# Routing attention and a squared-ReLU MLP on one core: the nine score tiles of a head pair in one run, its nine v products in another, and small transposes moved from TensorE to VectorE

## The chip, the cores and the metric

The kernel runs on one core of a Trainium2 chip. The time is device microseconds (us) of one launch, the median of several runs. Engines are named as the profile names them: PE (TensorE matmul) and PEld (its weight loads), DVE (VectorE), ACT (ScalarE), POOL (GpSimd) and SP (SyncE), whose queue issues nearly all DMAs in program order.

## The reference

Attention over 4 batches, 8 heads, 768 positions of 64 values; keys and queries see each other only if they fall to the same one of 16 clusters. An MLP follows.

```python
q_assign = argmax(einsum(q_n, c_n)); k_assign = argmax(einsum(k_n, c_n))
mask = q_assign[:, :, :, None] == k_assign[:, :, None, :]
scores = where(mask, scale * q @ k.T, -1e9)
attn = exp(scores - max); attn = attn / (sum(attn) + 1e-09)
x = (attn @ v) as (3072, 512)
out = square(maximum(x @ w_in, 0)) @ w_out        # 512 -> 2048 -> 512
```

## The kernel before, in words

**Attention** goes by pairs: two heads of a batch share the 128 partitions (64 values each), so there are NG = 16 pairs, p = 0 to 15. A pair's work on PE is: `logits` (L314; products with the centroids), `turn_logits` (L327; three 128x128 transposes), nine score tiles `sc` of 128 x 2 x 512, each made of products q.k (L435, f32) and of a mask product with one-hot cluster numbers `ohT` (L446, bf16), then 18 products with v (L521, into the bank `av`), and `add_up` (L533; sums of the exponentials over the keys, into `sm`). ACT makes each tile's exponential `ex` (L453, straight from PSUM) and evicts `av` into `xT` (L527). DVE and POOL add the exponentials of a pair into `total` (all under L456); DVE finds the cluster numbers from the logits (`number`, L347 to L360), inverts the sums (L543), multiplies x by them (`finish`, L556), and makes `ohT` (`one_hot`, L404 and L407).

A loop over t = 0 to 48 steps through thirds of pairs (p, ph = divmod(t, 3)): each step makes three score tiles, and then the v products of the step *before* it. Every engine runs in the order of the program text in this part (`manual_schedule`, closed at L688), so the text sets what is queued behind what.

Three things go through DRAM, all by SP. The raw q and k of pair p+3 are split into 16-bit halves by ACT (`flat`, L295), written (`words`, L296) and read back transposed (`qkT`, L307). The cluster numbers of a pair are written (`far`, L393) and read back spread over 2 x 64 partitions (`wide`, L396). The inverse sums are written (`far_r`, L546) and read back spread (`rb`, L549). Pairs 0 to 2 take their one-hots and pairs 0 and 1 their q, k by PE transposes instead.

PSUM: three score tiles of two banks each (`ps_sc`), one bank `av` (`ps_av`) and one bank for everything small (`ps_m`, "m").

**Weights** come in 32 blocks of 512 KB (16 of w_in, 16 of w_out), loaded into three buffers (L135) and rounded: `round_1` on ACT (L143, L144), `round_2` on DVE (L150, L153, L157), `round_3` on POOL (L165). Sixteen are rounded during attention, sixteen during the first `up`.

**The MLP** works by batches in the order 1, 2, 3, 0, each as `up` (L737: 8 groups of 7 products of 4 matmul rows, L748) and `down` (L766: 3 blocks of 7 products, L781), Strassen-like: sums of operands are made beforehand on POOL (`w_sums`, L586 and L566) and DVE (`x_sums`), and each product's bank is added into its results by DVE (`combine`, L723). Eight banks are in use here. In the first `up`, the hook `behind_group` adds up, inverts and finishes pair 15 and rounds two weight blocks in each group; before the first `down` the four sums `w_t` of w_out are made on DVE. From L688 on a scheduler orders the instructions.

Of the kernel before, what the change touches and what calls it, by code (L numbers as in the profile page):

```python
# [25 lines left out]
def kernel(  # L26
# [23 lines left out]
    NT = 3 * NG  # L50
# [13 lines left out]
    endp = ending.enter_context(tc.tile_pool(name="endp", bufs=2, side="right"))  # L64

    loads = att.enter_context(tc.tile_pool(name="loads", bufs=6))
# [5 lines left out]
    expp = att.enter_context(tc.tile_pool(name="expp", bufs=6))  # L72
# [11 lines left out]
    BY_PE, ONE_HOT = 2, 3  # L84
# [128 lines left out]
    seen = const.tile([4 * NG, TB], F32, name="seen")  # L213

    oh = once.tile([P, NB, 4, 2, D], BF16, name="oh")
    nc.gpsimd.memset(oh, 0.0)

# [96 lines left out]
    def logits(pair):  # L314
        hp = pair % HP
        lg = misc("lg", [P, TB], spare=pair == 0)
        for g in range(4):
            nc.tensor.matmul(  # L318
                lg[32 * g : 32 * g + 32], lhsT=cnT[:, 2 * C * hp : 2 * C * (hp + 1)],
                rhs=qkT[pair][:, NB * g : NB * (g + 1)], start=True, stop=True,  # L320
            )
        lgs[pair] = once.tile([P, TB], F32, name="lgs")
        nc.scalar.copy(out=lgs[pair], in_=lg)

    lts = {}

    def turn_logits(pair):  # L327
        lts[pair] = misc("lt", [P, NB, P])
        src = lgs.pop(pair)
        for i in range(NB):  # L330
            nc.tensor.transpose(  # L331
                out=lts[pair][:, i], in_=src[:, i * P : (i + 1) * P], identity=ident
            )

    numbers = {}

    def number(pair):
        n = NB * P // C
        mx = small.tile([P, n], F32, name="mx")
        best = once.tile([P, n, C], BF16, name="best")  # L340
        first = small.tile([P, n], F32, name="first")
        lt = lts.pop(pair).rearrange("p i (g c) -> p (i g) c", c=C)

        def over_c(t):
            return t.unsqueeze(2).to_broadcast([P, n, C])

        nc.vector.reduce_max(out=mx, in_=lt, axis=AX.X)  # L347
        nc.vector.tensor_tensor(out=best, in0=lt, in1=over_c(mx), op=ALU.is_ge)
        nc.vector.tensor_tensor(
            out=best, in0=best, in1=order.unsqueeze(1).to_broadcast([P, n, C]), op=ALU.mult  # L350
        )
        nc.vector.reduce_max(out=first, in_=best, axis=AX.X)
        if pair < ONE_HOT:
            nc.vector.tensor_tensor(
                out=oh.rearrange("p i g e c -> p (i g e) c")[:, :, 0:C], in0=best,
                in1=over_c(first), op=ALU.is_equal,
            )
        else:
            numbers[pair] = small.tile([P, 2, 4, NB], BF16, name="ids_b")
            nc.vector.tensor_copy(  # L360
                out=numbers[pair].rearrange("p e g i -> p i g e"),
                in_=first.rearrange("p (i g e) -> p i g e", i=NB, g=4),
            )

    def turn_onehot(pair):
        ohT[pair] = ohtp.tile([P, 2, S], BF16, name="ohT")
        for which in range(2):
            pt = misc("po", [P, NCH, P], BF16, spare=which == 0)
            for c in range(NCH):
                nc.tensor.transpose(  # L370
                    out=pt[:, c],
                    in_=oh[:, c % NB, 2 * which + c // NB].rearrange("p e c -> p (e c)"),
                    identity=ident_b,
                )
            dst = ohT[pair][:, which]
            src = pt.rearrange("p c n -> p (c n)")
            if which == 0:
                nc.vector.tensor_copy(out=dst, in_=src)
            else:
                nc.scalar.activation(out=dst, in_=src, func=ACT.Copy, bias=-BIG, scale=BIG)  # L380

    wide = {}

    def spread(pair):
        n = 8 * NB
        pb = misc("pb", [n, P], BF16)
        nc.tensor.transpose(
            out=pb, in_=numbers.pop(pair).rearrange("p e g i -> p (e g i)"), identity=ident_b
        )
        row = small.tile([n, P], BF16, name="row")  # L390
        far = dram.tile([2, n // 2, P], BF16, name="far")
        nc.scalar.copy(out=row, in_=pb)
        nc.sync.dma_start(far.rearrange("e r n -> (e r) n"), row)  # L393
        wide[pair] = once.tile([P, 2, S], BF16, name="wide")
        for e in range(2):
            nc.sync.dma_start(  # L396
                wide[pair][D * e : D * (e + 1)].rearrange("p g n -> p (g n)"),
                far[e].rearrange("r n -> (r n)").partition_broadcast(D),
            )

    def one_hot(pair):
        ohT[pair] = ohtp.tile([P, 2, S], BF16, name="ohT")
        src = wide.pop(pair)
        nc.vector.tensor_scalar(  # L404
            out=ohT[pair][:, 0], in0=src[:, 0], scalar1=cl, scalar2=None, op0=ALU.is_equal
        )
        nc.vector.tensor_scalar(  # L407
            out=ohT[pair][:, 1], in0=src[:, 1], scalar1=cl, scalar2=-BIG,
            op0=ALU.not_equal, op1=ALU.mult,
        )  # L410
# [6 lines left out]
    total = {}  # L417

    def pieces(t):
        pair, ph = divmod(t, 3)  # L420
        if ph < 2:
            rounds = [[(i, 3 * ph + i, slice(0, QA)) for i in range(3)]]
            queries = slice(0, QA)
        else:
            rounds = [[(i, 2 * i + j, slice(QB * j, QB * (j + 1))) for i in range(3)]
                      for j in range(2)]
            queries = slice(QA, S)
        return pair, rounds, queries

    def score_products(t, todo):  # L430
        pair, _, queries = pieces(t)
        for i, c, cols in todo:
            for e in range(2):
                rows = slice(D * e, D * (e + 1))
                nc.tensor.matmul(  # L435
                    sc[t][i][:, e, cols], lhsT=qkT[pair][rows, NCH + c],
                    rhs=qkT[pair][rows, queries.start // P : queries.stop // P],
                    start=True, stop=False,
                )

    def mask_products(t, todo):
        pair, _, queries = pieces(t)
        for i, c, cols in todo:
            for e in range(2):
                rows = slice(D * e, D * (e + 1))
                nc.tensor.matmul(  # L446
                    sc[t][i][:, e, cols], lhsT=ohT[pair][rows, 1, c * P : (c + 1) * P],
                    rhs=ohT[pair][rows, 0, queries], start=False, stop=True,
                )

    def exponential(t, i):
        ex.setdefault(t, []).append(expp.tile([P, 2, 512], F32, name="ex"))
        nc.scalar.activation(out=ex[t][i], in_=sc[t][i], func=ACT.Exp, scale=SCALE)  # L453
# [3 lines left out]

    part = {}

    def add_first(pair):  # L460
        e0, e1, e2 = ex[3 * pair]
        total[pair] = endp.tile([P, 2, S], F32, name="total")
        dst = total[pair][:, :, 0:QA]
        add(nc.vector, dst, e0, e1)
        add(nc.vector, dst, dst, e2)

    def add_second(pair):
        e0, e1, e2 = ex[3 * pair + 1]
        part[pair] = accp.tile([P, 2, 512], F32, name="part")
        add(nc.gpsimd, part[pair], e0, e1)  # L470
        add(nc.gpsimd, part[pair], part[pair], e2)

    def merge_second(pair):
        dst = total[pair][:, :, 0:QA]
        add(nc.vector, dst, dst, part.pop(pair))

    third = {}

    def add_third(pair):
        e0, e1, e2 = ex[3 * pair + 2]  # L480
        part[pair] = accp.tile([P, 2, 512], F32, name="part")
        add(nc.gpsimd, part[pair], e0, e1)
        third[pair] = e2

    def merge_third(pair):
        p = part.pop(pair)
        add(nc.vector, p, p, third.pop(pair))
        add(nc.vector, total[pair][:, :, QA:S], p[:, :, 0:QB], p[:, :, QB : 2 * QB])

    def begin(t):  # L490
        sc[t] = [ps_sc.tile([P, 2, 512], F32, name="sc") for _ in range(3)]

    def scores(t):
        begin(t)
        pair, rounds, _ = pieces(t)
        for todo in rounds:
            score_products(t, todo)
            if t % 3 == 0 and pair < ONE_HOT:
                turn_onehot(pair)
            mask_products(t, todo)  # L500
# [9 lines left out]
    def times_v(t):  # L510
        pair, rounds, queries = pieces(t)
        ph = t % 3
        if ph != 1:
# [522 lines left out]
```

## Time and profile before

| | us |
|---|---|
| median of 3 runs | 968.41 (966.81 to 968.68) |
| the profiled execution, own time | 964.27 |
| its span, first to last instruction | 962.4 |
| PE busy | 928.6 (96%) |
| DVE, ACT, POOL busy | 564.5, 319.9, 269.9 |
| granted TensorE clock, mean | 0.990 |
| attention, pair 0 to the first product of `up` | about 12 to 365.5 |
| first `up`, then first `down` | 365.5 to 447.4, to 522.4 |
| each later `up` and `down` | 72.24 and 72.52 |

In a timeline of the profile, a row has the start in us from the span's start, the duration in us, engine, line, operation, the tiles out<-in, the shape and how many instructions were merged; in brackets stands the idle time of the engine before it and what ended that. A PE row "64*128 64x512" is one pass of a matmul with 64 rows and 128 columns; an f32 matmul is two passes.

### The profile page before, as it was taken

The numbers are of one execution on the slowest core, as the hardware profiler recorded it, in microseconds if no ns is written. First come the engines' busy times: TensorE is split into PE (matmuls) and PEld (weight loads), VectorE is DVE, ScalarE is ACT, GpSimd is POOL, SyncE is SP. The second block draws the span as 40 slices with busy tenths as digits, with TensorE's granted clock in tenths as the row PEclk, the third lists the DMA queues.
The fourth block names the chain that finished last, engine by engine and source line by source line (L and its number), as shares of the span: only waits on it lengthen the run. The fifth ranks groups of instructions, "written<-read, shape, count | busy, mean of one in ns | idle before, by whom it ended". The sixth has DMA issues, their size and how long they took to land.

```text
span 962.4 us, 11697 instructions
## 1 busy us (share of the span) xinstructions
PE 928.6 (96%) x4556; PEld 585.8 (61%) x4556; DVE 564.5 (59%) x794; ACT 319.9 (33%) x491; POOL 269.9 (28%) x217
## 2 busy tenths in 40 slices
PE   8989999999999959988999999999999999999997
PEld 4444444444444425545887556887556888556886
DVE  5577886676668976988232666332666332666331
ACT  4757676666666534654000111000111000111000
POOL 0233444333444564671002320002321002321000
PEclk9999999999999988999999999999999999999999
DMA  6867787897775212421000000000000000000000
GB/s 199 229 136 183 193 237 191 211 209 191 197 194 160 94 40 73 146 84 65 22 22 23 0 1 1 23 22 22 1 0 1 22 22 22 0 1 1 22 23 26
DMA packets 97715, 79.66 MB, mean 83 GB/s; under 512 B 53493, under 2 KB 86645, under 8 KB 97397
## 3 DMA queue, kind: packets, MB, share of 16 engines
q1 hardware_dynamic: 95940, 78.41, 29.8%
q8 instruction: 38, 0.62, 0.3%
q10 hardware_dynamic: 1712, 0.43, 0.2%
q14 instruction: 25, 0.20, 0.1%
HBM read 48.66 MB, written 19.05 MB: 70 GB/s over the span
## 4 chain that ended last, share of the span: by engine, by line
PE 81%; DVE 8%; issue 4%; ACT 2%; DMA 2%; POOL 2%; ACTq 0%; SPq 0%; DVEq 0%; POOLq 0%
PE bank L781 29%; PE bank L748 23%; PE sc L435 11%; PE av L521 11%; PE sc L446 3%; DVE g L723 1%; PE lg L318 1%; PE sm L537 1%; DMA w_raw<-in_moe_w_out_dram 1%; DVE total L456 1%; DVE w_raw L150 1%; POOL w_out L165 1%; PE lt L331 1%; DVE w_raw L153 1%; DVE w_t L566 1%
## 5 line engine op out<-in xcount | busy, mean ns | idle before, releaser
L453 ACT ACTIVATE ex<-sc 128x1024 f32<-128x1024 f32 x144 | 140.2, 1025 | 87.6 <-PE sc L446 87.6
L723 DVE TENSOR_TENSOR g<-bank,g 128x384 f32<-128x384 f32 x192 | 103.5, 554 | 92.6 <-PE bank L748 89.1
L521 PE MATMUL av<-ex,v_raw 128*64 128x512 f32 (+1 forms) x768 | 137.0, 500 | 10.1 <-ACT xT L527 10.0
L435 PE MATMUL sc<-qkT 64*128 64x512 f32 (+1 forms) x768 | 140.9, 499 | 0.0
L456 POOL TENSOR_TENSOR part<-ex 128x1024 f32<-128x1024 f32 x32 | 77.2, 2412 | 206.5 <-ACT ex L453 180.9
L781 PE MATMUL bank<-w_out,g 128*128 128x256 f32 x576 | 127.2, 379 | 2.0 <-DVE g L566 2.0
L586 POOL TENSOR_TENSOR w_s<-w_in 128x256 f32<-128x256 f32 x32 | 26.3, 821 | 360.6 <-PE bank L781 242.0
L781 PEld LDWEIGHTS bank<-w_out,g 128*128 128x128 f32 x576 | 109.4, 190 | 18.1 <-DVE g L566 2.4
L723 DVE TENSOR_TENSOR osb<-bank,osb 128x256 f32<-128x256 f32 x72 | 29.5, 423 | 145.5 <-PE bank L781 134.9
L435 PEld LDWEIGHTS sc<-qkT 64*128 64x128 f32 x768 | 69.4, 188 | 56.4 <-issue 39.9
L521 PEld LDWEIGHTS av<-ex,v_raw 128*64 128x64 f32 x768 | 51.9, 139 | 80.4 <-issue 48.0
L748 PE MATMUL bank<-x_t,w_s 128*128 128x384 f32 x256 | 93.3, 487 | 1.8 <-POOL w_s L566 1.0
L748 PE MATMUL bank<-xT,w_in 128*128 128x384 f32 x256 | 93.8, 489 | 0.7 <-DVE g L723 0.7
L748 PE MATMUL bank<-xT,w_s 128*128 128x384 f32 x256 | 93.1, 486 | 1.2 <-DVE g L723 1.2
L781 PE MATMUL bank<-w_t,g_s 128*128 128x256 f32 x384 | 86.8, 379 | 0.0
L781 PE MATMUL bank<-w_t,g 128*128 128x256 f32 x384 | 86.8, 379 | 0.0
L781 PEld LDWEIGHTS bank<-w_t,g_s 128*128 128x128 f32 x384 | 73.0, 190 | 9.9
L781 PEld LDWEIGHTS bank<-w_t,g 128*128 128x128 f32 x384 | 73.0, 190 | 9.9
L727 ACT COPY osb<-bank 128x256 f32<-128x256 f32 x12 | 4.5, 372 | 213.5 <-PE bank L781 213.5
L748 PEld LDWEIGHTS bank<-x_t,w_s 128*128 128x128 f32 x256 | 48.4, 190 | 36.7 <-POOL w_s L566 1.6
L727 ACT COPY g<-bank 128x384 f32<-128x384 f32 x32 | 15.2, 475 | 165.4 <-PE bank L748 165.4
L748 PEld LDWEIGHTS bank<-xT,w_s 128*128 128x128 f32 x256 | 48.5, 190 | 35.5 <-DVE g L723 2.3
(122 smaller groups left out, 1057.6 us busy)
## 6 DMA issues: line engine op xcount, KB each, us to landing
words<-flat SPq DMA_DIRECT2D x28, 384.0 KB
w_raw<-in_moe_w_in_dram SPq DMA_DIRECT2D x16, 512.0 KB
w_raw<-in_moe_w_out_dram SPq DMA_DIRECT2D x16, 512.0 KB
v_raw<-in_v_dram SPq DMA_DIRECT2D x16, 384.0 KB
rb<-far_r SPq DMA_DIRECT2D x32, 192.0 KB
out_dram<-osb SPq DMA_DIRECT2D x23, 256.0 KB
q_raw<-in_q_dram SPq DMA_DIRECT2D x14, 384.0 KB
k_raw<-in_k_dram SPq DMA_DIRECT2D x14, 384.0 KB
```

Source lines behind the costliest of these rows:

```text
L150: nc.vector.scalar_tensor_tensor(out=lo, in0=hi, scalar=0x80000000, in1=lo, op0=ALU.bitwise_and, op1=ALU.bitwise_or)
L153: nc.vector.tensor_scalar(out=hi.bitcast(F32), in0=dst.bitcast(F32), scalar1=2.0 ** -15, scalar2=HIGHEST, op0=ALU.max, op1=ALU.min,)
L435: nc.tensor.matmul(sc[t][i][:, e, cols], lhsT=qkT[pair][rows, NCH + c], rhs=qkT[pair][rows, queries.start // P : queries.stop // P], start ...
L446: nc.tensor.matmul(sc[t][i][:, e, cols], lhsT=ohT[pair][rows, 1, c * P : (c + 1) * P], rhs=ohT[pair][rows, 0, queries], start=False, stop= ...
L453: nc.scalar.activation(out=ex[t][i], in_=sc[t][i], func=ACT.Exp, scale=SCALE)
L456: eng.tensor_tensor(out=out, in0=a, in1=b, op=ALU.add)
L521: nc.tensor.matmul(av[pair][D * e : D * (e + 1), 0:n], lhsT=raw_v[pair][:, e, c], rhs=e_t[i][:, e, cols], start=c == 0, stop=c == NCH - 1,)
L586: nc.gpsimd.tensor_tensor(out=s1, in0=a[1][0], in1=a[1][1], op=ALU.add)
L723: nc.vector.tensor_tensor(out=out, in0=bank, in1=to, op=ALU.add)
L727: nc.scalar.copy(out=c11, in_=bank)
L748: nc.tensor.matmul(bank, lhsT=operands[j][0][:, kk], rhs=operands[j][1][:, kk], start=(kk == 0), stop=(kk == H2 - 1),)
L781: nc.tensor.matmul(bank, lhsT=operands[j][0][:, f], rhs=operands[j][1][:, f], start=(f == 0), stop=(f == F2 - 1),)
```

## The change

1. **Order of a pair.** The loop goes by pairs. Tiles 0 to 5 (`tile_of`) are made one after another, each q.k product followed by its mask product; tiles 6 to 8 as before in two halves; then the v products of all nine. `expp` has 9 buffers instead of 6 (`loads` 5 instead of 6, `endp` 1 instead of 2). The second `av` bank is the small bank "m". Then come `logits` of pair p+2 and `add_up` of p itself.
2. **Transposes by DVE.** The logits are turned by DVE from PSUM in blocks of 32 x 32 (L335 of the changed kernel), without ACT's copy `lgs` and PE's `lt`. The cluster numbers are turned by DVE (L355), without PE's `pb` and ACT's `row`. The sums are turned by DVE and only one column in 32 is inverted (128x12 in place of 128x384). `wide` is filled for 16 of each 64 partitions; its buffer, and the inverses `seen`, are written in place, so that the copy `seen<-r` falls away. `far` and `far_r` become 128 rows of 64 and 48 bytes. Only pair 0 takes its one-hots by PE.
3. **Adds.** POOL adds tiles 0+1 and 3+4+5, DVE the rest; `finish` of pair p-1 stands in pair p between two adds of DVE, as two instructions, one for each half of the columns.
4. **Weights.** `round_1` of block p in pair p, `round_2` and `round_3` in pair p+1: one block in each pair, loaded two pairs ahead. 17 blocks are left for the first `up` (3, 3, 2, 2, 2, 2, 2, 1 by group).
5. **First `up` and first `down`** stay in the order of the text, until the first block of `down` is done. `round_1` stands behind the eviction of a group's first product, the squares of a group (all by ACT) in the next group, `w_sums` two groups ahead; the four sums `w_t` stand between the products of `down`.

The core of the loop after (the adds, weight rounds and the branches for p = 0 are cut):

```diff
+    for p in range(NG):
+        load_qk(p + 3)
+        load_ahead(0)
+        if p:
+            turn_words(p + 2)
+        load_v(p + 1)
...
+        if 2 < p + 1 < NG:
+            number(p + 1)
+        if p:
+            invert(p - 1)
...
+            for i in range(NB):
+                tile_of(p, i)
...
+        for i in range(NB, NCH):
+            tile_of(p, i)
...
+        split_words(p + 3, 0)
...
+        for i in range(NCH, NCH + NB):
+            exponential(i)
+        add(nc.vector, first, first, part)
+        if p:
+            finish(p - 1)
+            round_3(p - 1)
...
+        add(nc.vector, part, ex[NCH], ex[NCH + 1])
+        add(nc.vector, part, part, ex[NCH + 2])
+        add(nc.vector, last, part[:, :, 0:QB], part[:, :, QB : 2 * QB])
+        round_1(p)
...
+        bank = av_bank("av")
+        for i in range(NCH):
+            times_v(p, i, bank)
+        evict(p, 0, bank)
+        split_words(p + 3, 1)
+        bank = misc("av", [P, 512])
+        for i in range(NCH, NCH + NB):
+            times_v(p, i, bank)
+        raw_v.pop(p)
+        if 2 < p + 2 < NG:
+            logits(p + 2, misc("lg", [P, TB], spare=True))
+        evict(p, NCH, bank)
+        if p + 1 < NG:
+            add_up(p, misc("sm", [P, TB]))
+            one_hot(p + 1)
```

and what `add_up` left in PSUM is inverted one pair later:

```diff
+    def invert(pair):
+        turned = endp.tile([P, NBL, 32], F32, name="sums_t")
+        nc.vector.transpose(out=turned.rearrange("p b i -> p (b i)"), in_=sums.pop(pair))
+        r = seen[:, NBL * pair : NBL * (pair + 1)]
+        nc.vector.reciprocal(out=r, in_=turned[:, :, 0])
+        far = dram.tile([2, P // 2, NBL], F32, name="far_r")
+        nc.sync.dma_start(far.rearrange("e i b -> (e i) b"), r)
+        rb = endp.tile([P, 2, 32, NBL], F32, name="rb")
```

In the first `up`:

```diff
+            def behind_copy():
+                if waiting:
+                    squares(waiting.pop(), True)
+                rounding(i, 1)
...
+        if stage == 2 and i == 0:
             add_up(NG - 1, bank_tile(TB))
+            invert(NG - 1)
             finish(NG - 1)
```

## The prediction, made before the result was known

> **What bounds it now.** The page first: PE is busy 96% of the span and holds 81% of the chain that ended last, so I look for PE time saved and for the places where PE stood still.
>
> ```profile
> PE 928.6 (96%) x4556; PEld 585.8 (61%) x4556; DVE 564.5 (59%) x794; ACT 319.9 (33%) x491; POOL 269.9 (28%) x217
> PE 81%; DVE 8%; issue 4%; ACT 2%; DMA 2%; POOL 2%; ACTq 0%; SPq 0%; DVEq 0%; POOLq 0%
> ```
>
> Then PE's timeline. In mid attention it has no idle time; the pattern of 207.32 returns at 228.01, so a pair costs 20.69 us.
>
> ```profile
> 207.32 0.55 PE L331 MATMUL lt<-ident,lgs 128*128 128x128 f32 x3
> 207.80 2.85 PE L435 MATMUL sc<-qkT 64*128 64x512 f32 x12
> 210.48 0.81 PE L446 MATMUL sc<-ohT 64*128 64x512 bf16 x6
> 211.22 0.23 PE L387 MATMUL pb<-ident_b,ids_b 128*24 128x128 bf16 x1
> 211.38 2.81 PE L521 MATMUL av<-ex,v_raw 128*64 128x256 f32 x24
> ...
> 217.54 0.85 PE L537 MATMUL sm<-total,ups 128*32 128x384 f32 x8
> ```
>
> At the end of attention it stands still, in the same view, and ACT's timeline says why: an eviction is queued behind `round_1`, which waits for a weight block.
>
> ```profile
> 347.41 2.79 PE L521 MATMUL av<-ex,v_raw 128*64 128x512 f32 x12
> 360.21 5.39 PE L521 MATMUL av<-ex,v_raw 128*64 128x256 f32 x24 [10.01 <-ACT xT L527]
> 365.53 1.76 PE L748 MATMUL bank<-xT,w_in 128*128 128x384 f32 x4
> ```
>
> ```profile
> 359.04 0.65 ACT L144 ACTIVATE w_raw<-w_raw 128x512 f32<-128x512 uint32 x1 [8.88 <-DMA w_raw<-in_moe_w_out_dram]
> ```
>
> The 24 passes at 360.21 take 5.39 where 2.81 is usual: the granted clock of 340 to 380 is 0.83. The first `up` takes 365.53 to 447.40 = 81.87 against 72.24 later; the first `down` 74.95 against 72.52.
>
> Last SP's timeline, since the change puts its DMAs in another order:
>
> ```profile
> 207.70 0.39 SPq L296 DMA_DIRECT2D words<-flat  x1
> 208.13 0.56 SPq L104 DMA_DIRECT2D q_raw<-in_q_dram  x1
> 208.74 0.49 SPq L104 DMA_DIRECT2D k_raw<-in_k_dram  x1
> 210.95 4.05 SPq L307 DMA_TRANSPOSE qkT<-words  x1
> 215.04 0.57 SPq L135 DMA_DIRECT2D w_raw<-in_moe_w_in_dram  x1
> 215.72 0.34 SPq L393 DMA_DIRECT2D far<-row  x1
> 218.99 1.10 SPq L396 DMA_DIRECT2D wide<-far  x2
> ```
>
> Words wait 3.25 to land, the transposing DMA holds the queue 4 to 5 us, `far` to `wide` is 3.27.
>
> **PE's work for a pair after.** `lt` (0.48 from its start to the next) and `pb` (0.16) go. Between kinds of products PE loses about 0.1: 12 passes of q.k take 2.68 (12 x 512 columns at the spacing inside the block, 0.213, are 2.56), six mask products 0.74 (0.64). Going from q.k to mask and back loses nothing (222.45 to 222.78 is 0.33 for six of 256), so single tiles cost 0.853 + 0.213 = 1.07. Six of them, the last three in 3.25, v in 5.34 + 2.7, `lg` and `sm` 0.79 each, 0.1 for the entry: 19.4, against 20.69. Left to itself PE would win 1.3 a pair.
>
> **The new wait.** `finish(p-1)` now stands on DVE between the adds of pair p and waits for `rb`. Behind it on DVE: the adds of tiles 6 to 8, `total`, `one_hot(p+1)`; for these PE waits with `sm` and the first mask product of the next pair. `rb` comes from SP, which in pair p issues, in order: q and k of p+3, the transpose of p+2 (waits for the second words of pair p-1), v, `far`, `wide`, `far_r`, `rb`. Call m the start of a pair's first mask product.
>
> From m to the second words: 0.21 + 5 x 1.07, 0.5 wait of tile 8 for tile 5's exponential (exponentials start 0.91 apart), 3.25, v 5.34 = 14.65; eviction +0.12, next ACT start 0.48 later, two copies 1.58, issue 0.1: **16.9**.
>
> From there to the mask of the pair after next: 3.25 and 4.05 to 5.12 for the transpose (8.0 together), v 0.64, `far` to `wide` 2.7, two issues 1.16, `far_r` to `rb` 2.0, the second `rb` +0.52 and 3.70 to land (as `wide` at 199.97, awaited until 203.67): 18.7. Then `finish` 2 x 0.52 (half of 0.95 plus a start), adds 1.22 + 1.22 + 0.69, 0.1, `sm` 0.79 + 0.1, q.k 0.95: **24.85**.
>
> So two pairs take 41.75, **20.87 a pair**: what PE gains is lost to this chain, and PE idles 1.5 a pair before `sm`. Both unknown landings have ends: `far` to `wide` 1.32 (68.17, light queue) to 3.27 (4.57 once at 153.36), `far_r` to `rb` 1.78 (96.86) to 4.10 (5.09 once at 283.55). I take values nearer the light ends, as `far` now follows 384 KB in place of 512 and `far_r` follows a quarter of `wide`. The usual ends make 20.1 to 22.2. The number of rows, 128 of 48 bytes for 4 of 1.5 KB, has no row here; it is in these ends.
>
> A second loop, inside one pair: m, two exponentials (2.5), POOL 2.37, DVE and POOL in turn on tiles 2 to 5 and one weight block until about 13.7, `finish` and adds 4.2, `sm` and q.k 1.84: 19.8. It counts POOL and DVE as excluding each other where DVE has two SBUF inputs or a copy-like SBUF operation:
>
> ```profile
> 76.06 0.95 DVE L404 TENSOR_SCALAR ohT<-wide,cl 128x768 bf16<-128x768 bf16 x1
> 76.93 2.50 DVE L407 TENSOR_SCALAR ohT<-wide,cl 128x768 bf16<-128x768 bf16 x1
> ```
>
> The second has 0.41 when POOL rests (204.81); here POOL adds from 76.87 for 2.35.
>
> **Other edits.** The two DVE transposes of 128x384 have no row. Below, they can't be under the 0.55 of any DVE read of 384 f32 from PSUM (L347); above, I take the 2.56 of the slowest such row (L543); I use 0.56. Both lie beside PE: cluster numbers are then ready at m + 2.5, and SP comes to `far` at m + 4.7, so 2 us more are covered; beyond that each us costs half a us a pair. [...] Inverting 12 columns in place of 384 takes 2.4 from DVE, ACT loses two copies (0.72): both off the path, nothing counted. A quarter of `wide` is 0.3 MB less a pair; counted in the landings only.
>
> **Start.** First mask 16.1 (before 17.55, less `lgs` and `lt`). Pair 1's last q, k copy waits for ACT until 20.0, `lg`, tiles 3 to 5 to 24.2, exponentials to 25.3; then six copies of words (0.79 each) stand ahead of the last three exponentials, to 32.9; v to 35.6; words 36.3; `sm`: m = 38.5 for pair 1 (before 38.83). Pair 2: by words 36.3 + 8.65 + 2.0 + 4.2 + 4.3 + 1.84 = 57.3, by the inner loop 38.5 + 20 = 58.5. Before 65.59: **-7.1** (-4 to -9).
>
> **Pairs 2 to 14**: 12 x (20.87 - 20.69) = **+2** (-7 to +18). Before, the first mask of pair 14 is at 313.91, of pair 15 at 333.34; after 308.7 and, by the inner loop, 328.2.
>
> **End of attention.** From the mask of pair 15 to the first product of `up`: before 32.2, after 9.3 + 8.04 = 17.4: **-14.8**. Weights are now loaded two pairs ahead, so ACT doesn't wait. The cover is gone if a block is late again; then up to 12.6 (10.0 and the slow 2.6) come back.
>
> **First `up`.** 72.24 + `sm` 0.79. In group 0 `finish(15)` waits on DVE for `far_r` and `rb` (1.8 + 4.2 after about 1.8), then three blocks of `round_2` (1.55 each, in turn with POOL's 1.3): DVE is free for group 1 at about 14.5 us after group 0. PE has eight banks and is full at 0.8 + 9.03 + 2.6 = 12.4. Some 3 us of standing, 1 more for the next three-block group: 77.2 against 81.87: **-4.7** (-9 to +6).
>
> **First `down`.** The second product needs the last block (`round_2` 1.55, `round_3` 1.3 after the last add), the third needs DVE's 1.22 + 1.22 + 2.3 + 1.22 behind it: DVE 8.7 + squares 1.7 against two products, 6.9: 3.5 plus lag. 78 against 74.95: **+3** (0 to +6). The later batches: same work, 0.
>
> **Sum**: -7.1 + 2 - 14.8 - 4.7 + 3 = -21.6. On the profiled execution's 964.27 that is 942.7; the median of the runs shown is 4.1 above that execution, and I give the forecast on its scale: 968.4 - 21.6 = **946.8**.
>
> **Rivals.**
> A, the SP chain doesn't bind. For it: the transposing DMA takes 2.65 at 293.79, with no q, k ahead, and DMAs carry less. With that and light landings 38.1 for two pairs, so the inner loop's 19.6 rules: 12 x -1.27 = -15: 931.5. Against: q and k still stand just ahead of it. Chance 0.22.
> B, the first `up` gains nothing, because DVE's in-order wait for `rb` and POOL's turns keep PE's banks full in several groups: +11, 958. For it: DVE has 7 bank operations of 0.55 and 3.1 of rounding in 9.03, and POOL 5.6. Chance 0.14.
> C, slower: the SP chain is longer. Both landings at their loaded ends (4.57, 5.09) make 46.7 for two pairs, 23.4 a pair: +30, 977. It decides from 22.7 a pair, 3.6 us more in the chain. For it: these ends occur before; SP waits out each landing. Against: less is queued ahead. Chance 0.15.
> The forecast (940 to 954): 0.45. Smaller mixtures around no change: 0.04.
>
> The measurement can tell about 0.2% (1.9 us). Faster: forecast, A, B = 0.81, and 0.01 of the mixtures: 0.82; same 0.02; slower 0.16. The range reaches from A to the point where C begins to decide, and takes in 22.2 a pair (+16, 963): 930 to 965.
>
> **What will show it.** PE: single tiles 1.07 apart; idle before `sm` of about 1.5, ended by DVE; a pair of 20.9. DVE: `finish` waiting for `rb`. SP: the transpose 3.3 after words, `rb` 18.2 after words. No wait of ACT L143 for weights at attention's end; `up` in 77. Wrong would be: PE idle before the first mask rather than `sm`, a pair of 19.6 (A), ACT waiting for PE's scores with PE never idle, or waits of PE on banks throughout `up` (B).

## The result and the profile after

The changed kernel takes 965.28 us (median of 10 runs, 961.56 to 970.12), the kernel before 967.94 in the same comparison (10 runs, 965.23 to 968.68): a ratio of 0.9976, 95% interval 0.9954 to 0.9997. The forecast was 946.8, its range 930 to 965.0: a change of -21.6 had been forecast, -2.7 came.

The profiled executions were 964.27 before and 966.70 after: the one before lies 3.7 under its median, the one after 1.4 above. By them the change costs 2.4. The table goes by them, the medians decide on the whole.

| stage | before | after | difference | forecast |
|---|---|---|---|---|
| start to first mask product of pair 2 | 65.59 | 62.84 | -2.8 | -7.1 |
| from there to pair 14 | 248.32 | 261.48 | +13.2 | +2 |
| pair 14 to pair 15 | 19.43 | 24.01 | +4.6 | 0 |
| pair 15 to the first product of `up` | 32.19 | 17.67 | -14.5 | -14.8 |
| first `up` | 81.87 | 80.01 | -1.9 | -4.7 |
| first `down` | 74.95 | 78.7 | +3.8 | +3 |
| later batches | 434.4 | 434.4 | 0 | 0 |

The page of the changed kernel, the lines that answer to the first two shown of before:

```profile
PE 926.0 (96%) x4471; PEld 587.6 (61%) x4471; DVE 592.1 (61%) x849; ACT 314.4 (33%) x455; POOL 287.1 (30%) x218
PE 68%; DVE 15%; DMA 8%; issue 3%; ACT 2%; POOL 2%; SPq 1%; ACTq 0%; DVEq 0%
```

PE is as busy as before, but its share of the chain that ended last fell from 81% to 68%: DVE (8 to 15%) and DMAs (2 to 8%) took it. PE's timeline in two neighbouring pairs says where:

```profile
214.54 0.81 PE L467 MATMUL sm<-total,ups 128*32 128x384 f32 x2
215.55 0.85 PE L467 MATMUL sm<-total,ups 128*32 128x384 f32 x6 [0.20 <-DVE total L435]
...
235.36 0.81 PE L467 MATMUL sm<-total,ups 128*32 128x384 f32 x2
237.15 0.85 PE L467 MATMUL sm<-total,ups 128*32 128x384 f32 x6 [0.98 <-DVE total L435]
```

Eight passes into `sm` take 0.76 where nothing holds them up (118.64 in run 8 below). Here the first two start and the other six wait for DVE's last adds. The pairs that these rows close take 20.81 and 21.61, in turn. In DVE's timeline `finish` (L493) of the same two pairs is the cause:

```profile
209.62 2.68 DVE L493 SCALAR_TENSOR_TENSOR xT<-xT,rb 128x384 f32<-128x384 f32 x2
...
232.27 1.64 DVE L493 SCALAR_TENSOR_TENSOR xT<-xT,rb 128x384 f32<-128x384 f32 x2 [1.76 <-DMA rb<-far_r]
```

In the short pair `rb` is there, and `finish` takes 2.68, because POOL rounds a block (L165, 208.63 for 2.21) at the same time. In the long one it waits for `rb` first, and takes 1.64 after POOL is done.

Pair 5 is another thing. SP's timeline:

```profile
131.02 0.41 SPq L564 DMA_DIRECT2D x_far<-xT  x1
131.48 0.42 SPq L357 DMA_DIRECT2D far<-ids_t  x1
138.33 1.63 SPq L359 DMA_DIRECT2D wide<-far  x2
140.06 0.38 SPq L480 DMA_DIRECT2D far_r<-seen  x1
141.76 1.09 SPq L483 DMA_DIRECT2D rb<-far_r  x2
```

`far` stands behind the 1.5 MB of `x_far` and needs 6.83 to land where 3 is usual; SP waits for it, `rb` is late, DVE's `finish` waits 5.83 and PE 4.93: the pair takes 27.05. The busy times by window, for 145 to 150 and 150 to 155 (PE, PEld, DVE, ACT and POOL, then the granted clock, the DMA share and GB/s):

```profile
145.00:150.00 5.00, 0.85 (x6) 0.13 (x2) 3.93 (x4) 0.00 (x0) 0.00 (x0) 1.00 1.02 297
150.00:155.00 5.00, 4.22 (x16) 1.43 (x18) 4.76 (x11) 0.35 (x1) 0.00 (x0) 0.66 0.96 260
```

While PE stands the clock row still says 1.00; it is the stretch *after* the stall that has 0.66, so that this stall is paid a second time.

In the last two pairs DVE's `finish` and the add behind it are slow (3.26 and 1.76, where 1.64 and 1.22 are free):

```profile
337.41 3.26 DVE L493 SCALAR_TENSOR_TENSOR xT<-xT,rb 128x384 f32<-128x384 f32 x2
340.59 1.76 DVE L435 TENSOR_TENSOR part<-ex 128x1024 f32<-128x1024 f32 x1
```

beside POOL's four sums of w_in (L525, L505), of which this is the first:

```profile
338.61 1.36 POOL L525 TENSOR_TENSOR w_s<-w_in 128x256 f32<-128x256 f32 x1
```

PE then waits 2.11 for `total`, and the clock is 0.66 from 345 to 350. In the first `up` DVE waits for `rb` of pair 15 (3.58), then rounds three blocks, and PE's banks are full for 3.27.

### The profile page after: what moved, and what is told of

It reads as the page before. It is cut to its first block, busy times and chain, and to the rows that moved or that the text cites. A ratio compares the mean times of both kernels' runs of the same rounds, so it can differ in the third digit from the quotient of the medians.

```text
span 964.9 us, 11598 instructions
## 1 busy us (share of the span) xinstructions
PE 926.0 (96%) x4471; PEld 587.6 (61%) x4471; DVE 592.1 (61%) x849; ACT 314.4 (33%) x455; POOL 287.1 (30%) x218
## 4 chain that ended last, share of the span: by engine, by line
PE 68%; DVE 15%; DMA 8%; issue 3%; ACT 2%; POOL 2%; SPq 1%; ACTq 0%; DVEq 0%
PE bank L775 30%; PE bank L723 29%; PE sc L417 5%; DVE part L435 4%; DMA rb<-far_r 3%; DVE total L435 3%; DVE w_raw L150 2%; DMA far<-ids_t 2%; ACT ex L432 2%; POOL total L435 2%; DVE w_raw L153 2%; DMA far_r<-seen 2%; DVE xT L493 2%; PE sm L467 1%; PE av L449 1%
## 5 line engine op out<-in xcount | busy, mean ns | idle before, releaser
L432 ACT ACTIVATE ex<-sc 128x1024 f32<-128x1024 f32 x144 | 143.8, 1026 | 94.7 <-PE sc L425 90.8
L417 PE MATMUL sc<-qkT 64*128 64x512 f32 (+1 forms) x768 | 155.8, 505 | 5.0 <-ACT ex L432 5.0
L525 POOL TENSOR_TENSOR w_s<-w_in 128x256 f32<-128x256 f32 x32 | 24.7, 771 | 351.7 <-PE bank L775 228.1
L449 PE MATMUL av<-ex,v_raw 128*64 128x512 f32 (+1 forms) x768 | 127.4, 488 | 0.0
L417 PEld LDWEIGHTS sc<-qkT 64*128 64x128 f32 x768 | 71.5, 192 | 62.7 <-issue 46.4
L435 POOL TENSOR_TENSOR total<-ex 128x1024 f32<-128x1024 f32 x16 | 38.2, 2387 | 164.3 <-ACT ex L432 164.3
L723 PEld LDWEIGHTS bank<-xT,w_in 128*128 128x128 f32 x256 | 48.5, 190 | 37.6 <-DVE g L682 4.3
```

What stands on the lines that cost most here:

```text
L417: nc.tensor.matmul(sc[i][:, e, cols], lhsT=qkT[pair][rows, NCH + c], rhs=qkT[pair][rows, n.start // P : n.stop // P], start=True, stop=False,)
L432: nc.scalar.activation(out=ex[i], in_=sc.pop(i), func=ACT.Exp, scale=SCALE)
L435: eng.tensor_tensor(out=out, in0=a, in1=b, op=ALU.add)
L449: nc.tensor.matmul(bank[D * e : D * (e + 1), 0 : n.stop - n.start], lhsT=raw_v[pair][:, e, c], rhs=ex[i][:, e, cols], start=c == 0, stop=c ...
L525: nc.gpsimd.tensor_tensor(out=s1, in0=a[1][0], in1=a[1][1], op=ALU.add)
L723: nc.tensor.matmul(bank, lhsT=operands[j][0][:, kk], rhs=operands[j][1][:, kk], start=(kk == 0), stop=(kk == H2 - 1),)
```

## The experiments

Theory T is the prediction's, sharpened by the trace: a chain over SP and DVE closes over **two** pairs (42.4 us: in the table's stretch neighbouring pairs sum to 42.32 to 42.45 from pair 6 to 10); beside it turns of DVE and POOL cost 20.8 in each pair; single stalls come on top. The rivals are with each run. The time before was taken beside each group of four: 966.28, 968.92, 966.67.

**1. `finish` without its wait.**

```diff
-            finish(p - 1)
+            finish(p - 1, ex[0])   # in1 is a view of ex[0]
```

> In the pairs, finish multiplies x by a tile of exponentials in place of rb, so it does the same work on DVE and waits for no DMA; rb is still written and read back (the x values of pairs 0 to 14 are therefore not the reference's). Theory T: from the first mask product of one pair to that of the pair after next runs a chain over SP (words, transpose, far, wide, far_r, rb, finish) of 42.4 us; beside it the turns of DVE and POOL inside a pair take 20.8. Without the wait every pair costs 20.8 and the stall at pair 5 (first mask 126.97 to 154.02) goes: 12 x (21.2 - 20.8) = 5, 6.2 and some 1 at the start, 965.3 - 12 = 953. Rival R: the wait for rb is a symptom, and another wait (one-hots, transposed q and k) takes its place: 965, with PE idle before the first mask or before q.k.

953.99 us (0.9870, 0.9842 to 0.9898). Every pair from 2 to 13 takes 20.78 to 20.83, pair 5 too though `x_far` stands where it did, and PE's wait is the same in all:

```profile
205.14 0.85 PE L467 MATMUL sm<-total,ups 128*32 128x384 f32 x6 [0.18 <-DVE total L435]
...
225.95 0.85 PE L467 MATMUL sm<-total,ups 128*32 128x384 f32 x6 [0.18 <-DVE total L435]
```

So the wait for `rb`, not `finish` itself, made every second pair long and pair 5 very long. No other wait took its place.

**2. `x_far` later.**

```diff
-        if p == HP + 1:        # ahead of number(p + 1)
-            nc.sync.dma_start(x_far, xT.pop(0))
...
         split_words(p + 3, 0)
+        if p == HP + 1:
+            nc.sync.dma_start(x_far, xT.pop(0))
```

> Only the write of x_far (1.5 MB) moves on SP's queue from ahead of far to behind rb and the first words. T: far lands in about 3 instead of 6.8, the 5.83 us wait of finish in pair 5 shrinks to the usual 1 to 2, and 6.2 us go: 959. R: 1.5 MB hold the DMA engines wherever they stand, the second words land late and the next transpose with them: 963 to 965.

963.30 (0.9964, 0.9941 to 0.9988): no difference from the changed kernel that these intervals show. In the trace pair 5 falls from 27.05 to 21.83, but the next one rises from 20.94 to 23.45. DVE's `finish` in both:

```profile
141.74 1.62 DVE L493 SCALAR_TENSOR_TENSOR xT<-xT,rb 128x384 f32<-128x384 f32 x2 [2.05 <-DMA rb<-far_r]
...
165.21 1.61 DVE L493 SCALAR_TENSOR_TENSOR xT<-xT,rb 128x384 f32<-128x384 f32 x2 [3.68 <-DMA rb<-far_r]
```

The second words land after 5.68 and k after 6.52, and the next transpose starts late. T's 6.2 was wrong, the rival right: as long as the chain binds, the 1.5 MB cost time in both places tried. Over the two pairs it is 27.05 + 20.94 - 42.4 = 5.6 ahead of `far` and 21.83 + 23.45 - 42.4 = 2.9 here.

**3. `finish` one pair later.**

```diff
         nc.sync.dma_start(far.rearrange("e i b -> (e i) b"), r)
+        if pair:
+            finish(pair - 1)      # inside invert(pair); gone from the adds
         rb = endp.tile([P, 2, 32, NBL], F32, name="rb")
...
```

(`x_far` moves behind `rb` as well; it stands there in runs 7, 8, 11 and 12 too.)

> finish of pair p-1 moves from between the adds of pair p to pair p+1, behind the inversion of pair p, where DVE waits for POOL anyway; x_far goes behind rb with it. T: neither the SP chain nor finish stands ahead of the sums any more; PE's own 19.4 and its 0.7 at tiles 6 to 8 remain, 20.1 a pair: 12 x 1.1 = 13, 6.2 for x_far, 1 to 2 at the start, about 1.6 in each of the last two pairs: 943. R (POOL's three adds and DVE's rounding set the pair whatever finish does): 20.8 a pair, 953.

947.12 (0.9805, 0.9776 to 0.9835). Pairs 2 to 13 take 20.62 to 20.65 but for one of 20.77: the chain is gone, but the pairs did not fall to 20.1. DVE has next to no idle time left, because `finish` and the next add run beside POOL's adds:

```profile
185.79 3.78 DVE L495 SCALAR_TENSOR_TENSOR xT<-xT,rb 128x384 f32<-128x384 f32 x2
189.49 3.39 DVE L435 TENSOR_TENSOR total<-total,ex 128x1024 f32<-128x1024 f32 x1
```

```profile
185.83 3.03 POOL L435 TENSOR_TENSOR total<-ex 128x1024 f32<-128x1024 f32 x1 [7.59 <-ACT ex L432]
189.12 2.68 POOL L435 TENSOR_TENSOR part<-ex 128x1024 f32<-128x1024 f32 x1 [0.25 <-ACT ex L432]
```

In the changed kernel `finish` takes 1.64 behind POOL's work (232.27), and this add, begun ahead of POOL's next one, 1.23 (222.37); here they became 3.78 and 3.39.

**4. `round_3` to the start of the next pair.**

```diff
+        if p > 1:
+            round_3(p - 2)
         add(nc.gpsimd, first, ex[0], ex[1])
```

> round_3 moves from POOL's end of a pair (beside finish) to POOL's idle time at the start of the next. T: finish takes 1.6 instead of 2.7 where rb is there in time, but the two-pair chain stays 42.4, so a pair shorter by 1 is followed by one longer by 1: 964 to 965. R (each pair is set by its own DVE and POOL work): every other pair shorter by 1, 6 us less: 959.

965.48 (0.9969, 0.9947 to 0.9991). T's number came, but the run tells nothing about T, because the edit missed its place. POOL is idle at the end of a pair and the rounding waits only for DVE, so it ran where it ran before, beside `finish`, and the short pairs stayed at 20.80 to 20.84:

```profile
208.16 2.20 POOL L165 TENSOR_TENSOR w_in<-w_in,w_raw 128x512 int32<-128x512 int32 x1 [0.83 <-DVE w_in L157]
209.13 2.71 DVE L493 SCALAR_TENSOR_TENSOR xT<-xT,rb 128x384 f32<-128x384 f32 x2
```

**5. Sums of w_in at the start of the last pairs.**

```diff
+        if p >= NG - 2:
+            w_early.append(w_sums(len(w_early)))
         add(nc.gpsimd, first, ex[0], ex[1])
```

> The sums of w_in (four POOL operations) of pairs 14 and 15 move from the end of the pair, where they stand beside finish and the adds of tiles 6 to 8, to POOL's idle time at its start. T (DVE operations with two SBUF inputs and POOL's exclude each other): finish 3.26 becomes 2.7, the adds 1.76, 1.57 and 1.09 become 1.22, 1.23 and 0.69, PE no longer waits 2.11 before sm, and the granted clock of 0.66 that followed it goes: the last pair 24.0 becomes 21.2, 1 more at the first up: 961. Rival: at the pair's start POOL collides with the cluster numbers and far leaves later: 965.

967.72 (0.9995, 0.9973 to 1.0017): nothing gained. This edit missed its place too. POOL was idle and the sums wait for nothing in pair 14, so they ran right behind `round_3` of the pair before, again beside `finish`:

```profile
317.46 2.21 POOL L165 TENSOR_TENSOR w_in<-w_in,w_raw 128x512 int32<-128x512 int32 x1 [0.83 <-DVE w_in L157]
319.63 1.36 POOL L525 TENSOR_TENSOR w_s<-w_in 128x256 f32<-128x256 f32 x1
```

**6. `finish` of pair 15 behind the three rounded blocks.**

```diff
             invert(NG - 1)
-            finish(NG - 1)
...
+        if i == 0:             # behind the loop over the blocks
+            finish(NG - 1)
```

> In the first group of the first up, finish of pair 15 moves behind the three blocks that DVE rounds there. T: DVE's 3.58 wait for rb is filled with rounding, PE's 3.27 wait on full banks and the 1.9 lost to a lower clock behind it mostly go: first up 80.0 becomes 76, 961. Rival: rounding and POOL's turns alone fill the group, so PE's banks are full anyway: 964 to 965.

961.44 (0.9929, 0.9903 to 0.9954). The first `up` takes 75.9 in place of 80.0; DVE no longer waits for `rb`, and PE's longest wait for banks falls from 3.27 to 0.85.

**7. `finish` one pair later, beside an idle POOL.**

```diff
+        if p > 1:
+            finish(p - 2)
         if 2 < p + 1 < NG:
             number(p + 1)
```

> As the run with finish one pair later, but finish stands ahead of the cluster numbers, where POOL is idle, and not beside POOL's first add (where it took 3.78 and the add behind it 3.39). T: DVE gets about 3 us a pair back, PE is the bound with 19.4 and the 0.7 at tiles 6 to 8: 20.1 in place of 20.64 a pair, 947 - 13 x 0.55 = 940. Rival: far leaves 1.6 later, the one-hots with it, and PE waits at the first mask: 947 or more.

937.98 (0.9696, 0.9673 to 0.9719): pairs of 19.79 to 20.34, pair 14 of 20.05 with the sums of w_in where they were. One thing differs from run 3, the place of `finish` on DVE, and it is worth 9 us by the medians and 10 by the ratios. `finish` waits for `rb` here too, but POOL rests and it takes 1.60:

```profile
178.69 1.60 DVE L495 SCALAR_TENSOR_TENSOR xT<-xT,rb 128x384 f32<-128x384 f32 x2 [1.15 <-DMA rb<-far_r]
```

**8. All together.** Runs 5, 6 and 7, and:

```diff
+        bank = av_bank("av")
+        times_v(p, 0, bank)
         for i in range(NCH, NCH + NB):
             begin(i)
```

> The last three together, and the v products of tile 0 (0.9 us) moved to between tiles 5 and 6, where PE waits 0.68 for ACT's exponentials. T: 19.4 a pair, no stall in the last pairs, first up about 76: 940 - 1.5 - 4 - 14 x 0.65 = 925. Rival: DVE with POOL's turns is the bound at about 20 a pair: 933.

936.78 (0.9671, 0.9644 to 0.9698), 12 more than T said. Undisturbed pairs take 19.56, only 0.23 less than in run 7. PE doesn't wait in them, at the tiles or at `sm`:

```profile
118.64 0.83 PE L467 MATMUL sm<-total,ups 128*32 128x384 f32 x8
119.39 1.13 PE L417 MATMUL sc<-qkT 64*128 64x512 f32 x4
```

So PE's own work is the bound there, as T had it and not as the rival had it. Less is gained than the 0.68 at the tiles, because tiles 6 to 8 take 3.45 for 3.93, but the v products in two parts 8.13 for 7.89. The pairs from 7 to 14 are 7.1 over 19.56 together, and the largest takes 23.1: in pair 7, two after `x_far`, `finish` waits for `rb`, and the cluster numbers and PE (1.22 before the products of tile 0) wait behind it.

```profile
162.07 3.83 DVE L495 SCALAR_TENSOR_TENSOR xT<-xT,rb 128x384 f32<-128x384 f32 x2 [3.40 <-DMA rb<-far_r]
```

The rival's number is near (933), but not for its reason.

**9. The chain made longer.**

```diff
+            far_2 = dram.tile([2, P // 2, NBL], F32, name="far_2")
+            nc.sync.dma_start(far_2, far)
+            far = far_2
```

> The changed kernel with one hop more in the chain: far_r is copied to a second DRAM tile on SP, and rb reads that one. A hop is issue plus landing plus the wait of SP, about 2.1 by far_r to rb (1.7) and its own issue (0.42). T: the chain closes over two pairs, 42.4 + 2.1 = 44.5, so 1.05 a pair and not 2.1: 965.3 + 12.6 = 978, pairs of 20.8 and 23.7 in turn. Rival 1: every pair waits by itself, 2.1 each: 990. Rival 2: the chain has slack: 965.

978.74 (1.0118, 1.0086 to 1.0149). SP's timeline gives the price of the hop, 1.87 from its issue to that of `rb` (the tile is shown as `far`):

```profile
231.07 0.42 SPq L480 DMA_DIRECT2D far_r<-seen  x1
232.84 0.52 SPq L483 DMA_DIRECT2D far<-far_r  x1
234.71 1.10 SPq L487 DMA_DIRECT2D rb<-far  x2
```

Over 12 pairs the medians rose by 978.74 - 965.28 = 13.5, or 1.1 a pair: nearer to half of the hop (0.94) than to all of it, as a chain that closes over two pairs has it. The number alone would also fit a chain of one pair with 0.8 of slack; the order of the text and the pairs of 20.8 and 21.6 in turn speak for two. The pairs are less even than T's 20.8 and 23.7 (20.8 to 25.6 in a profiled execution of 984.69).

**10. The kernel before, with one order changed.** The rounding of the blocks of w_out on ACT stays behind the last eviction (`last_copy[0]`):

```diff
...
             n = next(to_round)
-            round_1(n)
+            with tc.issue_after(last_copy[0]):
+                round_1(n)
```

> The kernel before, with one thing changed: the rounding on ACT of the blocks of w_out may not be put ahead of the last eviction of av. T: the 10.0 us in which PE stands at the end of attention and the 2.6 of a lower clock behind them go, without anything of the new order of a pair: 968 - 12.6 = 955, so that the rest of the change costs some 10. Rival: the blocks rounded later come up again as waits in the first up: 962 to 966.

954.43 (0.9885, 0.9847 to 0.9923). PE's stall is 0.69 and its last products are at full speed, where 10.01 and 5.39 stood:

```profile
349.52 2.81 PE L521 MATMUL av<-ex,v_raw 128*64 128x256 f32 x24 [0.69 <-ACT xT L527]
```

From the first mask product of pair 15 to `up` it is 20.1. So 12.1 of the change's 14.5 there come from where ACT rounds, and the new order of a pair adds 2.4. The first `up` takes 83.6 in place of 81.87, a small part of what the rival had. This kernel is some 10 faster than the changed one.

**11. Runs 6 and 7 together.**

> The two moves of finish that helped, together: ahead of the cluster numbers of the pair after next, and in the first up behind the three roundings. T: they are in different stages and add up: 938 - 4 = 934, first up 77, pairs of 19.8.

934.51 (0.9677, 0.9647 to 0.9708): pairs of 19.79 to 20.32, first `up` 76.8, as expected.

**12. As run 11, with the products of tile 0 moved (run 8) and the weights behind the second words.**

```diff
         split_words(p + 3, 1)
+        load_ahead(p)
```

> As the run before, with the v products of tile 0 between tiles 5 and 6, and the weight block loaded behind the second words on SP's queue instead of ahead of them. T: in the run that had the former alone some pairs took 21 to 22, since words landed 6.6 after their issue behind a weight block and SP never caught up; with words first every pair takes 19.5: 934 - 14 x 0.25 = 930. Rival: SP's queue is late in any case once PE is faster: 935 or more.

935.70 (0.9693, 0.9654 to 0.9731): no better, as the rival had it. Words now land after 4.5, but q and k, behind the weights, take 7.2, the transposing DMA beside them 6.03, and `rb` is as late as in run 8. By these intervals runs 7, 8, 11 and 12 can't be told apart. The stages tell 7 and 11 apart: run 11's first `up` takes 76.8, run 7's 81.3, and the pairs are the same. So 11 is the version to keep, 3.2% under before and 20 us under run 10.

## Why the prediction was wrong

**PE's own work: right.** Single tiles are 1.07 apart (196.47, 197.54); 20.81 less the waits at `sm` (1.78 from its start to the next q.k, 0.76 without a wait) and at tiles 6 to 8 (3.93 for the forecast's 3.25) is 19.1 for the forecast's 19.4.

**The new wait: the mechanism was right, some sizes were short.** The first step, m to the second words, was 16.9 and is 17.0. From there to the mask of the pair after next it was 24.85 and is 25.4: `finish` takes 2 x 0.82 where the sum had 2 x 0.52. Two pairs 42.4 for 41.75. The inner loop was 19.8 and is 20.8 (run 1): `finish` takes 2.68 where the sum had 1.04, as its own time is 1.64 and `round_3` on POOL runs beside it, and the stretch ahead of it takes 13.15 for 13.7. That the rounding makes it slow is seen in the rows; run 4, meant to test it, left the rounding where it was. (Rival A and the start have this loop as 19.6 and 20; the sum of the pairs doesn't use it.) Run 1 shows the chain, and run 9 fits its length over two pairs.

**The step that failed** is the list of what SP issues in a pair: "q and k of p+3, the transpose of p+2 (waits for the second words of pair p-1), v, `far`, `wide`, `far_r`, `rb`". `x_far`, which the kernel before has at the same pair (L619, 134.75 there) and which delayed nothing then, wasn't in it. In the new order it stands ahead of `far`, on the chain: 27.05 - 21.2 = 5.9 in the profiled execution, and run 1 shows that it is paid through `rb`: there pair 5 takes 20.8. With 12 x (21.2 - 20.87) = 4.0 for the short sizes and 1.3 left for single late landings (in pair 11, of 22.43, `finish` waits 2.61) this is the +13.2 in place of +2. Where such a chain binds, a DMA that comes once belongs in the sum too.

It is the largest term, and not the only one. By the profiled executions 24.0 are missing: 11.2 in these pairs, 4.6 in pair 14, 4.3 at the start, 2.8 in the first `up` and 1.1 in the rest.

**Pair 14, counted at nothing, cost 4.6**: `finish` came to stand where POOL makes the sums of w_in, and PE's wait of 2.11 was followed by a clock of 0.66. That this is the cause is shown by the rows, by run 1 (still 23.23 without the wait for `rb`, `finish` in its place) and by run 7 (20.05 with `finish` elsewhere); run 5, meant to show it, did not. The price isn't fixed: in run 2, with the same order, `finish` was first (1.64), POOL's rounding took 4.86 and the pair 21.06, with no lower clock behind it.

**Start**: 4.3 of the 7.1 are missing. 1.1 stand ahead of the first mask (17.17 for 16.1), which moves from one execution to the next (15.48 to 17.49 in runs 1 to 6). Pair 1 takes 23.72 for 20: it has `number(2)` beside POOL's adds (L337 2.27 and L340 2.60 for 0.56), `finish` beside `round_3` (2.72), and 0.65 for a mask pass of 0.38 after PE's wait of 1.77: each in the trace, none tried alone. Without `finish` in it (runs 3 and 7) pair 1 takes 21.84 and 21.86.

**End of attention**: -14.5 for -14.8, right, and run 10 shows that most of it needed none of the new order. **First `up`**: -1.9 for -4.7; the wait for `rb` (3.58) was seen, but not the slow passes behind PE's stall (2.31 and 2.44 for 1.45). Run 6 gives both back. **First `down`** +3.8 for +3. **DVE's transposes** 0.54 to 0.58 for the 0.56 taken (0.21 for the numbers), and off the path as said.

**Rivals**: A is refuted by the trace and run 1, C did not come (it needed 22.7 a pair, the mean is 21.8). B's wait was there once, in one group, and the first `up` is 2.8 over the forecast where B had 11.

## What to carry to other kernels

When an instruction that waits for a DMA is put between others on an in-order engine, follow its chain until it closes: here over two pairs, so that about half of a delay on it was paid in each (1.1 of 1.87 in run 9), and a 1.5 MB transfer that was free before cost 3 to 6. Where the consumer of such a DMA has a pair of time, put it a pair later (some 18 us here, with `x_far` moved too), and choose the place by what the *other* engine does then: the same instruction was worth some 9 us more beside an idle POOL. When you move an instruction, see in the trace whether it moved: on an idle in-order engine it may run where it ran before, as on POOL in runs 4 (208.16) and 5 (319.63). And before crediting a new order with a one-off stall that it removes, try removing the stall alone: it took one condition in the kernel before and gave more than the whole change.

## What the runs showed of the hardware

PE's granted clock falls after short waits, though not after all. Behind waits of 2.11 (345.21) and 4.93 (150.78) in the changed kernel it was 0.66 from 345 to 350 and from 150 to 155, behind 1.77 (60.76) 0.71 from 60 to 65, and four q.k passes took up to 2.08 for 1.13. Behind 0.98 (237.15) they took 1.13; behind 1.43 in run 8 (180.85) and 2.06 in run 5 (326.25) they took 1.13 too, and the clock was 1.00 from 180 to 185 and from 326 to 331. The first row is the changed kernel's, the second run 5's:

```profile
345.00:350.00 5.00, 4.79 (x20) 1.78 (x22) 3.37 (x7) 0.94 (x1) 0.00 (x0) 0.66 0.03 5
...
326.00:331.00 5.00, 4.75 (x28) 2.02 (x30) 4.48 (x11) 2.48 (x3) 0.35 (x1) 1.00 0.03 5
```

So the length of a wait alone doesn't decide: 1.77 was followed by a lower clock and 2.06 was not. What decides was not shown.

The prediction counts some operations of DVE and POOL as excluding each other, and rows show them so: the one that starts later takes longer. Beside POOL's adds DVE's `best<-lt,mx` (L337, two inputs from SBUF) took 2.72 for 0.56 (181.41 in run 7) and the copy-like `w_raw<-w_in` (L153) 2.49 for 0.43 (205.57 in the changed kernel); beside DVE's add POOL's rounding took 2.21 (208.63), where 1.30 stood in the kernel before (203.38). Other operations of DVE took no longer beside POOL's add of 184.62 in run 7: 0.56 for a reduction (L350, 184.76), 0.54 for the transpose from PSUM (L476, 185.49).

An idle in-order engine didn't keep an instruction for the place that the text gives it: POOL ran the sums of run 5 a pair early, from 319.63, and the rounding of run 4 at 208.16, at the end of the pair before.
